# Longer loads in rows of 48 KB, and copies, gelu scaling and row sums on ScalarE, in a one-core adaLN decode kernel

## The chip, the core and the metric

The kernel runs on one NeuronCore of one Trainium2 chip. The core has TensorE (PE in the profile; PEld is its weight load), VectorE (DVE), ScalarE (ACT), GpSimd (POOL) and SyncE (SP), which here does nothing but issue transfers from HBM; 16 DMA engines carry them. PSUM is the memory that TensorE writes, SBUF the working memory of all engines. The metric is the device time of one execution in microseconds (us), the median over several runs. A difference of 2% (7.7 us) is called faster or slower.

## What is computed

One decode step of a transformer block for B = 4 rows of D = 512 values: adaptive layer norm, attention of 32 query heads over 8 cached key/value heads with 4096 positions each, an output projection, a second adaptive layer norm, and a token-mixing MLP with 1792 hidden units. All is fp32.

```python
mod = (_silu(c) @ w_mod).reshape(c.shape[0], 6, 1, -1)
sa, ca, ga, sb, cb, gb = (mod[:, 0], mod[:, 1], mod[:, 2], mod[:, 3], mod[:, 4], mod[:, 5])
h = _layernorm(x, axis=-1) * (1 + ca) + sa
x = x + ga * _A_ref(h, A_k_cache, A_v_cache, A_wq, A_wo)
h = _layernorm(x, axis=-1) * (1 + cb) + sb
x = x + gb * _B_ref(h, B_w1, B_b1, B_w2, B_b2)
...
scores = jnp.einsum("bhqd,bhkd->bhqk", q, k) * (Dh ** -0.5)
p = _softmax(scores, axis=-1)
o = jnp.einsum("bhqk,bhkd->bhqd", p, v)
...
u = jnp.einsum("bsd,sf->bdf", h, w1) + b1
u = _gelu(u)
y = jnp.einsum("bdf,fs->bds", u, w2) + b2
```

The caches hold 4 x 8 = 32 pairs of a key tile K and a value tile V, each 128 partitions by 4096 fp32 values, 16 KB in each partition and 2 MB in all. The kernel reads each once: 128 MB of its 157 MB.

## The kernel before

**Heads.** The unit of work is a "head" i = 0 to 31, a pair of batch row b = i // 8 and key/value head h = i % 8. For head i the score matmuls `s` (L231) read K_i, VectorE takes the row maximum (`m`, L236), TensorE turns it (`pm`, L240), VectorE takes the maximum over the four column groups (`mx`, L245), TensorE spreads it with its sign changed (`pb`, L251), VectorE copies it from PSUM to SBUF (`nm`, L256), and ScalarE computes the exponential with its sum (`p`, L261). VectorE transposes p (L267), TensorE multiplies it with V_i (`pv`, L291), and VectorE copies the product to SBUF (`po`, L314). Then TensorE gathers the head's output (`pt`, L328, called the pick here), multiplies it with the output weights (`pa`, L343), and VectorE adds it up (`acc`, L361).

**The loop.** For i = 0 to 23 a loop runs these steps staggered. Iteration i has, in TensorE's order: the scores of head i+2, the pick, the sums and the projection of head i-1, the turn of the maximum of head i+2, the first half of the values of head i, the spread `pb` of head i+2, and the second half of the values of head i. The pv tile in PSUM has one buffer, and so the values of head i+1 start only when `copy_v(i)` has emptied it; the pick of head i reads that copy. The last eight heads run in an order written out by hand, the string `PLAN`, whose letters are looked up in two tables.

**The mixer.** The MLP of batch row b runs inside the loop while the heads of row b+1 are attended: `Mixer.inner(k)` and `Mixer.outer(k)` with k = i % 8 add a piece to each iteration (i = 8 to 15 for row 0, 16 to 23 for row 1; row 2 is in `PLAN`, row 3 behind it). For k = 3, 4, 5 in `inner`, and k = 2 to 5 in `outer`, `both()` makes one tile of hidden units: `expand` (two VectorE instructions, scale and bias, L442) and `gelu` (one ScalarE instruction of 1024 elements per partition, L506). `inner` stands ahead of the second half of the values and of `copy_v(i)` in the program, `outer` behind. The exponential and gelu need different ScalarE tables, so ScalarE has an ACT_TABLE_LOAD at each change.

**Loads.** All loads go through one queue, SP's. A ring of three slots of 32 KB per partition (`ring`, bufs=3) takes 4 MB loads: `load_first` K0 and K1, then `load_pair(i)` K(i+2) and V(i) side by side in rows of 32 KB. A slot is free when both its tiles are read. In the last stage `PLAN` places the loads (LP, LT, LK, LV, LW). The output weights come in four loads of 2 MB (`wo_p`), the weights of the modulations in three groups (`wmod`).

**Where the last heads fold the gate.** `fold_gate` multiplies eight slices of the output weights with the gate and takes row sums of the result in one VectorE instruction each (L592).

Of the kernel before, what the change touches and what calls it, by code (L numbers as in the profile page):

```python
# [8 lines left out]
F32 = mybir.dt.float32  # L9
AF = mybir.ActivationFunctionType  # L10
OP = mybir.AluOpType
# [13 lines left out]
NARROW = NS - 3  # L25


@with_exitstack
def adaln_decode(ctx: ExitStack, tc: tile.TileContext, small, x, wmod, wq, kk, kv, vv, wo, out):
# [12 lines left out]
    mm = nc.tensor.matmul  # L42
    dv = nc.vector
# [4 lines left out]
    wm01 = ring.tile([P, 2, 4, D], F32, name="wm01", tag="kv")  # L48
    nc.sync.dma_start(wm01, wmod[0])
    nc.sync.dma_start(sm, small)  # L50
    nc.sync.dma_start(xr, x)
    wqt = []
    for k in range(0, 4, 2):
        t = ring.tile([P, 2, HQ * DH], F32, name=f"wq{k}", tag="kv")
        nc.sync.dma_start(t, wq[k // 2])
        wqt += [t[:, 0], t[:, 1]]
    w1, b1, w2 = sm[:, 0:NF], sm[:, NF:2 * NF], sm[:, 2 * NF:3 * NF]
# [33 lines left out]
    wo_p = [wos.tile([P, 2, REP, D], F32, name=f"wo{h}") for h in range(0, HKV, 2)]  # L91
    wo_t = [wo_p[h // 2][:, h % 2] for h in range(HKV)]
# [64 lines left out]
    KT, VT, WM = {}, {}, {}  # L157

    def slots():
        return ring.tile([P, 2, SK], F32, name="kv", tag="kv")  # L160

    def key(t, i):
        KT[i] = t

    def value(t, i):
        VT[i] = t.rearrange("p (j d) -> p j d", d=DH)

    def load_first():
        t = slots()
        nc.sync.dma_start(t, kk)  # L170
        key(t[:, 0], 0)
        key(t[:, 1], 1)

    def load_pair(i):
        t = slots()
        nc.sync.dma_start(t, kv[i])
        key(t[:, 0], i + 2)
        value(t[:, 1], i)

    def load_wo(h):  # L180
        nc.sync.dma_start(wo_p[h // 2], wo[h // 2])

    def load_wm24():
        w = ring.tile([P, 3, 4, D], F32, name="wm24", tag="kv")
        nc.sync.dma_start(w[:, 0:2], wmod[1])
        nc.sync.dma_start(w[:, 2], wmod[2][:, 0])
        for e in range(3):
            WM[2 + e] = w[:, e]

    def load_wm5():  # L190
        t = slots().rearrange("p s (k n) -> p (s k) n", n=D)
        nc.sync.dma_start(t[:, 0:4], wmod[2][:, 1])
        WM[5] = t[:, 0:4]
        return t[:, 4:6]

    def load_key(t, i):
        nc.sync.dma_start(t, kv[i - 2][:, 0])
        key(t, i)

    def load_v(t, i, cuts):  # L200
        value(t, i)
        src = (kv[i][:, 1] if i < NS - 2 else vv[i - NS + 2]).rearrange("p (j d) -> p j d", d=DH)
        for lo, hi in zip(cuts, cuts[1:]):
            nc.sync.dma_start(VT[i][:, lo:hi], src[:, lo:hi])
# [21 lines left out]
    def scores(i):  # L226
        b, h = divmod(i, HKV)
        S[i] = s = ps_s.tile([P, 1024], F32, name=f"s{i}", tag="s")
        for n in range(2):
            for c in range(4):  # L230
                mm(s[32 * c:32 * c + 32, n * 512:(n + 1) * 512], QT[:, b, h, :],  # L231
                   KT[i][:, (n * 4 + c) * 512:(n * 4 + c + 1) * 512], start=True, stop=True)

# [20 lines left out]
    def copy_max(i):  # L254
        nm = wk.tile([P, 1], F32, name="nm")
        dv.tensor_copy(nm, M[i])  # L256
        M[i] = nm
# [27 lines left out]
    def values(i, ks):  # L285
        if ks[0] == 0:
            PV[i] = ps_v.tile([P, 4 * DH], F32, name="pv", tag="pv")
        pT = PL[i][0]
        for k in ks:
            q = k % 4  # L290
            mm(PV[i][32 * q:32 * q + 32, :], pT[:, 128 * k:128 * k + 128:4],  # L291
               VT[i][:, 4 * k:4 * k + 4, :].rearrange("p j d -> p (j d)"), start=(k < 4), stop=(k >= 4))

    def values_narrow(i, ks, pv=None):
        if ks[0] == 0:
            PV[i] = ps_v.tile([P, DH], F32, name="pvn", tag="pv") if pv is None else pv
        pv = PV[i]
        pT = PL[i][0].rearrange("p (k r) -> p k r", r=32)
        top = 32 if i < NS - 1 else 30
        for k in ks:  # L300
            for j in range(4 * k, min(4 * k + 4, top)):
                c = j % 4
                mm(pv[32 * c:32 * c + 32, :], pT[:, j, :], VT[i][:, j, :], start=(k == 0), stop=(j + 4 >= top))  # L303

# [32 lines left out]
    def project(i, pa=None, between=None):  # L337
        b, h = divmod(i, HKV)
        oT = OT[i]
        if pa is None:  # L340
            pa = ps_m.tile([P, D], F32, name="pa", tag="m")
            for g in range(REP):
                mm(pa[32 * g:32 * g + 32, :], oT[:, g:g + 1].to_broadcast([P, 32]), wo_t[h][:, g, :],  # L343
                   start=True, stop=True)
        else:
            for g in range(REP):
                for c in range(4):
                    mm(pa[32 * c:32 * c + 32, :], oT[:, g:g + 1].to_broadcast([P, 32]),  # L348
                       wo_t[h][:, g, c * P:(c + 1) * P], start=(g == 0 and h == HKV - 2),
                       stop=(g == REP - 1 and h == HKV - 1))  # L350
# [105 lines left out]
    class Mixer:  # L456
# [52 lines left out]
        def both(self, u=None):  # L509
            self.expand(u)  # L510
            self.gelu()
# [40 lines left out]
    def finish(b, pg, py, hb, wr):  # L552
        uu = ring.tile([P, 16, D], F32, name="uu", tag="kv")
# [55 lines left out]
    load_first()  # L609
    load_pair(0)  # L610
    load_wo(0)
# [6 lines left out]
    for i in range(NS - HKV):  # L618
        load_pair(i + 1)
        if i in (1, 3, 5):  # L620
            load_wo(i + 1)
        if i == 1:
            load_wm24()
# [25 lines left out]
        if i == 2:  # L649
            for t in range(2, 5):  # L650
                pm = mod(t)
                dst = prep[:, {2: 1, 3: 2, 4: 3}[t]]
                if t == 4:
                    dv.tensor_scalar(dst, pm, 1.0, None, op0=OP.add)
                else:
                    nc.scalar.activation(dst, pm, AF.Copy)
        if i == NS - HKV - 2:
            gate = spread_gate()
# [4 lines left out]
    pve = pgx = pc = ep = spare = slot = None  # L663
    gates = list(range(2 * REP))
    cuts = {NS - 1: (0, 16, 24, 28, 30, 32), NS - 2: (0, 16, 32)}
    last, halves = [(0, 1, 2, 3), (4, 5), (6,), (7,)], [(0, 1), (2, 3), (4, 5), (6, 7)]
    PLAN = """
    a23 v24.0 A23 p23 t25.0 P23 F R v24.1 LP25 G s26 t25.1 M H V24 LP26 Q a24 S26 v25.0 N s27 x A24 f p24 g
    x LP27 m26 S27 P24 m27 X26 X27 b26 B26 e26 x b27 v25.1 c g t26.1 l25 t26.0 B27 s28 V25 c g L25
    v26.0 v26.1 S28 x l26 f a25 L26 V26 A25 x m28 p25 LT X28 e27 c a26 P25 t27.0 A26 b28 s29 f B28 p26 e28  # L670
    LK30 t27.1 S29 P26 v27.0 m29 l27 g LK31 T t28.1 X29 LT t28.0 s30 L27 S30 b29 v27.1 B29 e29 l28 m30 V27
    LV28 L28 a27 g X30 t29.1 t29.0 l29 L29 s31 A27 LV29 b30 p27 x B30 S31 c c m31 e30 P27 X31 v28.0 f LT LV30
    b31 v28.1 B31 f e31 LV31 l30 V28 L30 t30.1 l31 L31 a28 t31.1 A28 p28 v29.0 v29.1 t30.0 f P28 V29 v30.0 a29
    v30.1 A29 LW p29 f v30.2 v30.3 t31.0 P29 g V30 Y y a30 A30 p30 E x v31.0 f v31.1 v31.2 v31.3 V31 z31 a31 I A31 j p31
# [3 lines left out]
             "l": sums, "L": scale, "V": copy_v, "a": pick, "A": copy_o, "P": add_up,  # L678
             "LP": load_pair}
# [4 lines left out]
    for step in PLAN.split():  # L684
# [19 lines left out]
        elif op == "LT":  # L704
            slot = slots()
        elif op == "LK":
            load_key(slot[:, i % 2], i)
        elif op == "LV":
            load_v(slot[:, i % 2], i, cuts.get(i, (0, 32)))
        elif op == "LW":  # L710
            spare = load_wm5()
        elif op == "x":
            mix.expand(spare if mix.n == 6 else None)
# [75 lines left out]
```

## Time and profile before

| | |
|---|---|
| Time, median of 3 runs | 386.43 us (386.31 to 390.96) |
| Span of the profiled execution, first to last instruction | 384.7 us |
| Median run less that span | 1.8 us |
| Mean granted TensorE clock | 0.883 |
| HBM read | 157.32 MB, 409 GB/s over the span |
| Busy: PE, DVE, ACT | 298.7, 198.2, 112.2 us |

The profile is one execution. Its own time as a run is not listed; its span is 1.8 us under the median time, and the work in the argument below is set against the span. Of an engine the page gives busy time and, for each group of instructions, the idle time ahead of them with what ended it. A wait is put down to what came last. The rows that matter are quoted in the prediction.

### The profile page before, as it was taken

Reading aid. Unit: us, or ns where it says so; the run is one execution under the profiler, and the core shown is the slowest. Engines: PE = TensorE matmul, PEld = TensorE weight load, DVE = VectorE, ACT = ScalarE, POOL = GpSimd, SP = SyncE. Lnnn points to the kernel's source line nnn. Section 1 sums busy time; section 2 is a strip of 40 time slices with the busy share of each in tenths; the row PEclk is TensorE's granted clock in tenths of the full one; section 3 lists DMA queues with packets and bytes.
Section 4 is the critical chain, followed back from the end, with each engine's and each line's share of the span. In section 5 each row is a group of like instructions: output and inputs, shape, how many; then the busy total and the mean of one; then the engine's idle time right before and its main releaser. Section 6 shows DMA issues by size and latency. Waiting matters only on the chain.

```text
span 384.7 us, 5604 instructions
## 1 busy us (share of the span) xinstructions
PE 298.7 (78%) x2380; PEld 117.2 (30%) x2380; DVE 198.2 (52%) x407; ACT 112.2 (29%) x144; POOL 7.7 (2%) x33
## 2 busy tenths in 40 slices
PE   0856777866966949979877878788888887999984
PEld 0112122311323313334322222342222343333653
DVE  1130251620451424664866545557665567778757
ACT  1001111121110110212567311124575105657276
POOL 1100000000000000000000000000000000000000
PEclk9989555985695685998999998999999999999999
DMA  8999999999999999999999999999999999999930
GB/s 331 433 433 436 411 453 433 409 432 436 423 441 433 434 436 436 434 436 431 429 425 433 428 433 434 429 433 431 429 434 436 434 436 432 424 417 423 418 122 3
DMA packets 7409, 157.69 MB, mean 410 GB/s; under 512 B 964, under 2 KB 1236, under 8 KB 1496
## 3 DMA queue, kind: packets, MB, share of 16 engines
q1 hardware_dynamic: 7376, 157.33, 95.4%
q8 instruction: 18, 0.29, 0.3%
q14 instruction: 7, 0.06, 0.0%
q10 hardware_dynamic: 8, 0.00, 0.0%
HBM read 157.32 MB, written 0.01 MB: 409 GB/s over the span
## 4 chain that ended last, share of the span: by engine, by line
DMA 60%; PE 29%; DVE 7%; ACT 2%; issue 1%; POOL 0%; SPq 0%; POOLq 0%; DVEq 0%
DMA kv<-in_kv 58%; PE s L231 8%; PE pv L291 7%; PE s L122 2%; PE qs L138 2%; DVE m L236 2%; DVE p L267 2%; DMA sm<-in_small 2%; PE pa L343 2%; PE pt L328 2%; ACT uu L562 1%; PE pb L251 1%; PE pve L303 1%; PE pm L240 1%; PE pgx L348 1%
## 5 line engine op out<-in xcount | busy, mean ns | idle before, releaser
L231 PE MATMUL s<-kv,QT 128*32 128x512 f32 x512 | 75.2, 714 | 38.9 <-DMA kv<-in_kv 37.0
L236 DVE TENSOR_REDUCE m<-s 128x1 f32<-128x1024 f32 x32 | 39.2, 1224 | 96.0 <-PE s L231 95.9
L261 ACT ACTIVATE p<-s,nm 128x1024 f32<-128x1024 f32 x32 | 35.7, 1115 | 180.6 <-DVE nm L256 180.5
L291 PE MATMUL pv<-kv,p 128*32 128x512 f32 x464 | 69.8, 670 | 0.7 <-DMA kv<-in_kv 0.7
L231 PEld LDWEIGHTS s<-kv,QT 128*32 128x32 f32 x512 | 15.8, 123 | 84.0 <-DMA kv<-in_kv 52.5
L328 PEld LDWEIGHTS pt<-g,po 128*128 128x128 f32 x236 | 31.1, 205 | 27.2 <-issue 19.9
L343 PE MATMUL pa<-wo,oT 128*32 128x512 f32 x240 | 34.6, 648 | 4.6 <-DVE oT L335 4.4
L328 PE MATMUL pt<-g,po 128*128 128x4 f32 (+2 forms) x236 | 33.9, 267 | 1.5 <-DVE po L314 1.0
L267 DVE STREAM_TRANSPOSE p<-p 128x1024 f32<-128x1024 f32 x25 | 30.9, 1234 | 0.0
L314 DVE COPY po<-pv 128x512 f32<-128x512 f32 x29 | 20.0, 688 | 16.8 <-PE pv L291 16.7
L245 DVE TENSOR_REDUCE mx<-pm 1x128 f32<-1x512 f32 x32 | 21.3, 669 | 1.1 <-PE pm L240 1.1
L442 DVE TENSOR_SCALAR u<-hb,wr,sm 128x512 f32<-128x512 f32 x40 | 19.9, 541 | 1.9 <-POOL wr L437 1.0
L506 ACT ACTIVATE u<-u 128x1024 f32<-128x1024 f32 x20 | 20.4, 1051 | 1.5 <-DVE u L442 1.4
L361 DVE TENSOR_TENSOR acc<-acc,pa 128x512 f32<-128x512 f32 x26 | 17.8, 686 | 4.3 <-PE pa L343 4.2
L261 ACT ACT_TABLE_LOAD x11 | 14.1, 1283 | 20.3 <-DVE nm L256 20.2
L251 PEld LDWEIGHTS pb<-neg,mx 1*128 1x128 f32 x64 | 10.4, 202 | 28.2 <-DVE mx L245 26.5
L122 PE MATMUL s<-wm,sT 128*4 128x512 f32 x16 | 9.1, 732 | 10.6 <-DVE sT L108 10.6
L506 ACT ACT_TABLE_LOAD x13 | 16.7, 1283 | 0.2
L291 PEld LDWEIGHTS pv<-kv,p 128*32 128x32 f32 x464 | 13.4, 146 | 7.2 <-issue 3.1
L240 PE MATMUL pm<-ident,m 128*1 128x128 f32 x32 | 9.3, 289 | 7.4 <-DVE m L236 3.5
L251 PE MATMUL pb<-neg,mx 1*128 1x1 f32 x64 | 13.1, 271 | 2.1 <-DVE mx L245 2.1
L453 PE MATMUL py<-u,sm 128*32 128x512 f32 x80 | 14.4, 616 | 0.0
(158 smaller groups left out, 214.7 us busy)
## 6 DMA issues: line engine op xcount, KB each, us to landing
kv<-in_kv SPq DMA_DIRECT2D x28, 4096.0 KB, 21.9
wq<-in_wq SPq DMA_DIRECT2D x2, 4096.0 KB, 16.3
wo<-in_wo SPq DMA_DIRECT2D x4, 2048.0 KB
kv<-in_kv SPq DMA_DIRECT2D x4, 2048.0 KB, 20.3
wm<-in_wmod SPq DMA_DIRECT2D x2, 2048.0 KB, 14.8
kv<-in_kk SPq DMA_DIRECT2D x1, 4096.0 KB
kv<-in_vv SPq DMA_DIRECT2D x3, 1024.0 KB
wm<-in_wmod SPq DMA_DIRECT2D x1, 1024.0 KB
```

The lines of the kernel that those rows point to most:

```text
L231: mm(s[32 * c:32 * c + 32, n * 512:(n + 1) * 512], QT[:, b, h, :], KT[i][:, (n * 4 + c) * 512:(n * 4 + c + 1) * 512], start=True, stop=True)
L236: dv.tensor_reduce(M[i], S[i], axis=AX.X, op=OP.max)
L245: dv.tensor_reduce(mx, M[i].rearrange("o (c r) -> o r c", c=4).unsqueeze(1).to_broadcast([1, 4, 32, 4]), axis=AX.X, op=OP.max)
L251: mm(pb, M[i].rearrange("o c r -> o (c r)"), neg1, start=True, stop=True)
L261: nc.scalar.activation(p, S[i], AF.Exp, bias=M.pop(i), accum_out=l)
L267: dv.transpose(PL[i][0], PL[i][0])
L291: mm(PV[i][32 * q:32 * q + 32, :], pT[:, 128 * k:128 * k + 128:4], VT[i][:, 4 * k:4 * k + 4, :].rearrange("p j d -> p (j d)"), start=(k < ...
L314: dv.tensor_copy(PV[i], pv)
L328: mm(pt, po[:, c * DH:(c + 1) * DH], sel.unsqueeze(1).to_broadcast([P, m, REP]), start=(c == 0), stop=(c == n - 1))
L343: mm(pa[32 * g:32 * g + 32, :], oT[:, g:g + 1].to_broadcast([P, 32]), wo_t[h][:, g, :], start=True, stop=True)
L442: dv.tensor_scalar(u[:, e, :], hb, wr[:, j:j + 1], b1[:, j:j + 1], op0=OP.mult, op1=OP.add)
L506: nc.scalar.activation(u, u, AF.Gelu_apprx_tanh)
```

## The change

**Loads.** The ring becomes one tile of six 16 KB tiles (`RING`), and a list made by `queue()` gives the order of the loads. `kk` (K0, K1) is followed by 14 loads `kvk` of three tiles each in rows of 48 KB: by turns K(m+2), V(m), K(m+3), and V(m+1), K(m+4), V(m+2), with m = 0, 3, ..., 18. They cover V0 to V20 and K2 to K22. Then come seven pairs of 32 KB rows, K30, K31 and V28 to V31 one by one, and the last modulation weights. A load is issued as soon as the program has passed the last reader of each tile that it overwrites: `advance(name)` is called behind the last reader. The ring thus holds two loads of three tiles where it held three loads of two.

**Weights.** The output weights come in two loads of 4 MB instead of four of 2 MB. Modulation weights 0 and 1, and later 2 to 4, are loaded into the place of output weights that come behind them, so they no longer take a ring slot. The matmuls of modulations 2 to 4 (`mod`) move from the end of iteration 2 to the end of iteration 1.

**Engines.** `copy_max` (all heads), `copy_v` (heads 0 to 23) and the first `add_up` of each batch row move from VectorE to ScalarE. `both()` loses its two VectorE instructions; ScalarE does scale, bias and gelu in two instructions of 512. `fold_gate` becomes a VectorE multiply of 1024 per partition for the first four calls and a ScalarE copy with a row sum for all eight.

```diff
-    ring = ctx.enter_context(tc.tile_pool(name="ring", bufs=3))
+    ring = ctx.enter_context(tc.tile_pool(name="ring", bufs=1))
...
+    RING = ring.tile([P, 6, SK], F32, name="kv")
+    wo_t = wos.tile([P, HKV, REP, D], F32, name="wo")
+    wm01, wm24 = wo_t[:, 0:2], wo_t[:, 4:7]
...
+    def queue():
+        q = [entry(["K0", "K1"], kk)]
+        for n in range(NT):
+            m = n // 2 * 3
+            names = [f"V{m + 1}", f"K{m + 4}", f"V{m + 2}"] if n % 2 else [f"K{m + 2}", f"V{m}", f"K{m + 3}"]
+            q.append(entry(names, kvk[n]))
+        for i in range(NP, NS - 4):
+            q.append(entry([f"K{i + 2}", f"V{i}"], kv[i - NP]))
...
+        q.insert(2, ("wo", "M0", wo_t[:, 0:4], wo[0]))
+        q.insert(4, ("wo", None, wm24, wm2))
+        q.insert(6, ("wo", "M2", wo_t[:, 4:8], wo[1]))
+        return q
...
+    def advance(name=None):
+        read.add(name)
+        while LOADS:
...
+                if any(h not in read for h in held[p:p + n]):
+                    return
...
     def copy_max(i):
         nm = wk.tile([P, 1], F32, name="nm")
-        dv.tensor_copy(nm, M[i])
+        nc.scalar.activation(nm, M[i], AF.Copy)
...
     def copy_v(i):
         pv = PV[i]
         PV[i] = wk.tile(list(pv.shape), F32, name="po")
-        dv.tensor_copy(PV[i], pv)
+        if i < NS - HKV:
+            nc.scalar.activation(PV[i], pv, AF.Copy)
+        else:
+            dv.tensor_copy(PV[i], pv)
...
-            dv.tensor_copy(ACC[b], pa)
+            nc.scalar.activation(ACC[b], pa, AF.Copy)
...
-        def both(self, u=None):
-            self.expand(u)
-            self.gelu()
+        def both(self):
+            u = up.tile([P, 2, D], F32, name="u")
+            js = (2 * self.n, 2 * self.n + 1)
+            for e, j in enumerate(js):
+                nc.scalar.activation(u[:, e], self.hb, AF.Gelu_apprx_tanh, bias=b1[:, j:j + 1],
+                                     scale=self.wr[:, j:j + 1])
+            self.done.append((u, js))
+            self.n += 1
...
     def fold_gate(gate, es):
-        for e in es:
-            w = wo_t[HKV - 2 + e // REP][:, e % REP]
-            dv.tensor_tensor_reduce(w, w, gate, 1.0, 0.0, OP.mult, OP.add, rowsum[:, e:e + 1])
+        for n in es:
+            if n < REP:
+                w = wo_t[:, HKV - 2 + n // 2, n % 2 * 2:n % 2 * 2 + 2]
+                dv.tensor_mul(w, w, gate.unsqueeze(1).to_broadcast([P, 2, D]))
+            w = wo_t[:, HKV - 2 + n // REP, n % REP]
+            nc.scalar.activation(w, w, AF.Copy, accum_out=rowsum[:, n:n + 1])
...
-        load_pair(i + 1)
-        if i in (1, 3, 5):
-            load_wo(i + 1)
-        if i == 1:
-            load_wm24()
...
-        if i == 2:
+        if i == 1:
             for t in range(2, 5):
...
-    x LP27 m26 S27 P24 m27 X26 X27 b26 B26 e26 x b27 v25.1 c g t26.1 l25 t26.0 B27 s28 V25 c g L25
+    x m26 S27 P24 m27 X26 X27 b26 B26 e26 x b27 v25.1 c g t26.1 l25 t26.0 B27 s28 V25 c g L25
```

ScalarE's order in the iterations with a mixer piece, before: the exponential `p` and the gelu `u` take turns, with a table load ahead of each.

```order
L506 ACT_TABLE_LOAD
L506 ACTIVATE u<-u 128x1024 x2
L261 ACT_TABLE_LOAD
L261 ACTIVATE p,l<-s_1088,nm 128x1024
L506 ACT_TABLE_LOAD
```

The same place after the change:

```order
L271 ACTIVATE nm<-pb 128x1
L276 ACT_TABLE_LOAD
L276 ACTIVATE p,l<-s_1493,nm 128x1024
L535 ACT_TABLE_LOAD
L535 ACTIVATE u<-hb,sm,wr 128x512 x2
L334 ACTIVATE po<-pv 128x512
L535 ACTIVATE u<-hb,sm,wr 128x512 x2
```

The copy `nm` now stands ahead of the exponential, and the copy `po` of the values stands behind the exponential, a table load and the two gelu instructions of `inner`.

TensorE's order of the same iterations before, with the engine that each row waits for (DMAHW is a load):

```order
L231 MATMUL s_1023<-kv,QT 32x512 [waits DMAHW0_49]
L231 MATMUL s_1023<-kv,QT 32x512 x7
L328 MATMUL pt<-g_122,po 128x4 [waits DVE_49]
L328 MATMUL pt<-g_122,po 128x4 x3
L275 MATMUL pl<-g_122,l 128x4 [waits Activation_49]
L343 MATMUL pa<-wo_129,oT 32x512 [waits DVE_49]
```

and after:

```order
L245 MATMUL s_1493<-kv,QT 32x512 x8
L350 MATMUL pt<-g_121,po 128x4 [waits Activation_49]
L350 MATMUL pt<-g_121,po 128x4 x3
L290 MATMUL pl<-g_121,l 128x4
L365 MATMUL pa<-wo,oT 32x512 [waits DVE_49]
```

The pick `pt`, which waited for VectorE's copy, now waits for ScalarE's (Activation).

SP's queue from the first key load on, before (up to the first long run of pairs):

```order
L170 DMA kv<-in_kk 128x8192
L176 DMA kv<-in_kv 128x8192
L181 DMA wo_128<-in_wo 128x4096
L176 DMA kv<-in_kv 128x8192 x2
L181 DMA wo_129<-in_wo 128x4096
L185 DMA wm_337<-in_wmod 128x4096
L186 DMA wm_337<-in_wmod 128x2048
```

and after:

```order
L210 DMA kv<-in_kk 128x8192
L210 DMA kv<-in_kvk 128x12288
L192 DMA wo<-in_wo 128x8192
L210 DMA kv<-in_kvk 128x12288
L192 DMA wo<-in_wm 128x6144
L210 DMA kv<-in_kvk 128x12288
L192 DMA wo<-in_wo 128x8192
L210 DMA kv<-in_kvk 128x12288 x11
L210 DMA kv<-in_kv 128x8192 x7
```

The 45 transfers of the new queue carry the same bytes as the 55 of the old one.

More of the change, by code (lines that the diff above doesn't have):

```diff
@@ L155, in adaln_decode @@
     nc.scalar.activation(prep[:, 0], px, AF.Copy)
[L157 to L204, printed above, removed]
+    KT, VT, WM = {}, {}, {2 + e: wm24[:, e] for e in range(3)}
+    held, read = [("Q", 0), ("Q", 0), ("Q", 1), ("Q", 1), None, None], {None, ("Q", 0), ("Q", 1)}
@@ new lines, in adaln_decode @@
+    LOADS, at = queue(), [4]
+    def advance(name=None):
+        read.add(name)
+        while LOADS:
+            kind, names, *rest = LOADS[0]
+            if kind == "wo":
+                if names not in read:
+                    return
+                nc.sync.dma_start(*rest)
+            else:
+                n, p = len(names), at[0]
+                if any(h not in read for h in held[p:p + n]):
+                    return
+                for k, nm in enumerate(names):
+                    t, i = RING[:, p + k], int(nm[1:])
+                    if nm[0] == "K":
+                        KT[i] = t
+                    elif nm[0] == "V":
+                        VT[i] = t.rearrange("p (j d) -> p j d", d=DH)
+                    else:
+                        WM[i] = t.rearrange("p (k n) -> p k n", n=D)[:, 0:4]
+                held[p:p + n] = names
+                at[0] = (p + n) % 6
+                if names[0] == "W5":
+                    nc.sync.dma_start(WM[5], rest[0])
+                elif len(names) > 1:
+                    nc.sync.dma_start(RING[:, p:p + n], rest[0])
+                elif names[0][0] == "K":
+                    nc.sync.dma_start(RING[:, p], rest[0])
+                else:
+                    cs = cuts.get(i, (0, 32))
+                    v = rest[0].rearrange("p (j d) -> p j d", d=DH)
+                    for lo, hi in zip(cs, cs[1:]):
+                        nc.sync.dma_start(VT[i][:, lo:hi], v[:, lo:hi])
+            LOADS.pop(0)
@@ L552, in finish @@
     def finish(b, pg, py, hb, wr):
-        uu = ring.tile([P, 16, D], F32, name="uu", tag="kv")
+        uu = RING[:, 4:6].rearrange("p s (k n) -> p (s k) n", n=D)
         for js in ((0,), (1,), (2, 3, 4), (5, 6, 7), (8, 9, 10), (11, 12), (13,)):
```

77 lines of the change are left out of this document (42 added, 35 removed).

## The prediction

> **What bounds the kernel now.** I read the page's slices and queues first, then the chain of waits, then who waits late in the program.
>
> ```profile
> span 384.7 us, 5604 instructions
> ...
> DMA  8999999999999999999999999999999999999930
> GB/s 331 433 433 436 411 453 433 409 432 436 423 441 433 434 436 436 434 436 431 429 425 433 428 433 434 429 433 431 429 434 436 434 436 432 424 417 423 418 122 3
> ...
> q1 hardware_dynamic: 7376, 157.33, 95.4%
> ...
> kv<-in_kv SPq DMA_DIRECT2D x28, 4096.0 KB, 21.9
> ```
>
> The 16 DMA engines are full from the first slice to the 39th at some 433 GB/s. The loads are the bound, and bytes don't change; what can be won on them is small, and each microsecond in which the queue stands empty is lost. The chain of waits gives the pace:
>
> ```profile
> 201.31 1.97 PE s L231 x16
> ...
> 208.57 21.85 DMA kv<-in_kv
> 230.47 3.32 PE s L231 x16
> ...
> 260.73 1.97 PE s L231 x16
> ...
> 289.74 1.97 PE s L231 x16
> ```
>
> These starts of scores wait for a pair's landing and lie three heads apart: 29.0 us, 9.67 for a head, 4.84 for a tile of 2 MB. Last, the waits of TensorE from 289 us to 372 us:
>
> ```profile
> PE s L231 <- DMA kv<-in_kv: 2.2, 2, 1.6
> ...
> PE pv L291 <- DMA kv<-in_kv: 0.7, 2, 0.5
> ```
>
> Of these 2.9 us, 1.6 are the wait at 289.74 itself. Behind it TensorE waits 1.3 us for loads until the end: whatever makes it late at head 24 makes the end late, less 1.3.
>
> **The new wait.** In iterations 11, 12, 13 and 19, 20, 21 ScalarE copies the values only behind `inner`'s gelus, and the next pick needs that copy. TensorE's part at full clock (timeline; pick, spread, second half of the values, MLP matmuls):
>
> ```profile
> 201.31 1.92 PE L231 MATMUL s<-kv,QT 128*32 128x512 f32 x16 [1.70 <-DMA kv<-in_kv]
> 203.16 1.06 PE L328 MATMUL pt<-g,po 128*128 128x4 f32 x8
> ...
> 206.07 1.10 PE L291 MATMUL pv<-kv,p 128*32 128x512 f32 x8
> 207.11 0.38 PE L251 MATMUL pb<-neg,mx 1*128 1x1 f32 x2
> 207.42 1.10 PE L291 MATMUL pv<-kv,p 128*32 128x512 f32 x8
> 208.33 1.04 PE L453 MATMUL py<-u,sm 128*32 128x512 f32 x8
> ```
>
> Scores to pick 1.85; pick to the end of the spread 207.49 - 203.16 = 4.33; pick to the last read of V 5.36. ScalarE's part, by groups and two timeline rows:
>
> ```profile
> L261 ACT ACTIVATE p<-s,nm 128x1024 f32<-128x1024 f32 x32 | 35.7, 1115 | 180.6 <-DVE nm L256 180.5
> L506 ACT ACT_TABLE_LOAD x13 | 16.7, 1283 | 0.2
> ...
> L261 ACT ACTIVATION_READ_ACCUMULATOR p<-s,nm 128x1 f32 x32 | 6.2, 193 | 0.0
> ...
> L218 ACT ACTIVATE ym<-pm 128x512 f32<-128x512 f32 x3 | 1.8, 597 | 7.8 <-PE pm L215 7.8
> L557 ACT ACTIVATE uu<-hb,sm,wr 128x512 f32<-128x512 f32 x2 | 1.5, 806 | 0.1
> ...
> L416 ACT ACTIVATE sd<-ph,epsc 128x1 f32<-128x1 f32 x1 | 0.3, 261 | 0.5 <-PE ph L737 0.5
> ```
>
> ```profile
> 267.19 1.28 ACT L261 ACT_TABLE_LOAD   x1 [4.59 <-DVE nm L256]
> ...
> 268.48 1.11 ACT L261 ACTIVATE p<-s,nm 128x1024 f32<-128x1024 f32 x1
> ```
>
> Copy of the maximum 0.26 (nearest row: one column, 261 ns), table load 1.28, exponential with its sum 1.31, table load 1.28, two scaled gelus 1.5 (their rows overlap), copy of the values 0.60, hand-overs 0.1: 6.33. The load of the exponential's table stood idle until `nm` was there; the order after has it behind `nm` too, so it stays in the ring of waits. Pick to pick takes 4.33 + 6.33 = 10.66 us, against 9.67 of the stream. Behind the waiting pick stand the projection, the turn of the maximum and the next values on TensorE; behind `nm` on ScalarE everything that ScalarE does, which is why the turns are serial. `outer`'s gelus come behind the copy, in the shadow of TensorE's 4.33.
>
> The Trainium skill, ScalarE: Activation LUTs, section "What ACT_TABLE_LOAD costs", has a drain of some 1380 ns beside the 1283 ns of every switch. The trace doesn't agree: 267.19 + 1.28 is 268.47, and the exponential starts at 268.48. By the page each turn would take 2.8 us more, a rival below.
>
> **The ring.** At the median a pair landed 21.9 us after its issue, 9.7 of them its own: it was issued with 12.2 us of work still queued. Two loads of three tiles leave less; behind a load that SP holds back stand all later loads. What a late issue costs:
>
> ```profile
> 0.72 0.39 SPq L49
> ...
> 1.18 7.60 DMA sm<-in_small
> ```
>
> The first slice (9.62 us) moved 331 of 433 GB/s, so 2.27 us of it are empty; less 0.72, 1.5 us lie between issue and first bytes. The first load and `small` are 2.13 MB, 4.9 us; 2.2 + 4.9 = 7.1, but `small` landed at 8.78: a landing comes 1.7 us behind the last byte.
>
> Now along the stream, first mixer. The score at 201.31 waits for K15 and V13. Afterwards [K14,V12,K15] lands one tile earlier, at 196.5, and head 14's scores start there. Picks: 198.3; spread's end 202.7, copy 209.0 = next pick; 219.7 the third; V14 is read at 225.0. The load after the next two goes over V14. Those two end in bytes at 196.5 + 29.0 - 1.7 = 223.8; its own start at 226.5: an empty queue for 2.7 us.
>
> Second mixer, without that gap. 260.73 is K21's landing with V19; afterwards [K20,V18,K21] lands at 255.9. Head 20's scores, once possible at 251.1, start there; head 21's 8.8 us later (251.1 to 259.8 before), 264.7. V19 comes with the next load, 255.9 + 14.5 = 270.4. Spread's end 271.8, copy and pick 278.2, then 288.8 and 299.5. Before, that last pick stood here:
>
> ```profile
> 291.59 1.05 PE L328 MATMUL pt<-g,po 128*128 128x4 f32 x8
> ```
>
> So it is 7.9 us late; with the gap 10.6; less 1.3 of slack, 9.3 at the end.
>
> **The clock.** In each turn TensorE has 1.85 + 5.36 + 0.95 = 8.2 us of work in 10.66 and idles 2.5. Idle times and granted clock before:
>
> ```profile
> 172.23 3.37 PE L231 MATMUL s<-kv,QT 128*32 128x512 f32 x16 [1.88 <-DMA kv<-in_kv]
> ...
> 230.47 3.26 PE L231 MATMUL s<-kv,QT 128*32 128x512 f32 x16 [2.46 <-DMA kv<-in_kv]
> ```
>
> ```profile
> 141.00:154.70 13.70, 11.45 (x53) 4.21 (x57) 4.04 (x7) 0.73 (x1) 0.00 (x0) 0.50 1.03 442
> ...
> 171.80:175.20 3.40, 2.97 (x16) 0.60 (x16) 0.02 (x1) 0.00 (x0) 0.00 (x0) 0.50 0.96 414
> ...
> 229.80:233.20 3.40, 2.73 (x16) 0.59 (x16) 0.00 (x0) 0.00 (x0) 0.00 (x0) 0.50 1.00 434
> ```
>
> Behind idle times of 1.88 and 2.46 us the clock (third column from the end) was 0.50 for 3.4 us, and elsewhere for 13.7 at a stretch; 1.70 us (201.31) did nothing. At that clock pick to spread's end is longer:
>
> ```profile
> 122.43 1.87 PE L328 MATMUL pt<-g,po 128*128 128x4 f32 x8
> ...
> 128.69 0.58 PE L251 MATMUL pb<-neg,mx 1*128 1x1 f32 x2
> ```
>
> 129.27 - 122.43 = 6.84, 2.5 more. Six turns: 0 to 15 us; half of them slow, 7.5. The two-load ring also has longer idle stretches and no reserve at that clock: in the plain heads, 120 to 190 us, a load must be issued 14.5 - 1.7 - 1.5 = 11.3 us behind a landing, its last reader ends at 7.2 + 1.9 = 9.1 at full clock and, if the span from pick on stretches by 6.84/4.33, at some 14.4: up to 3 us of empty queue for each drop there, and two or three drops: 0 to 9, I take 2.5. Together 10, between 0 and 24.
>
> The Trainium skill, TensorE: Matmul & The Clock Gate, Part 1, has the clock halve after at least one idle window of some 3.4 us. The rows show halving after 1.88 us without work. By the page the 2.5 us of a turn would leave the clock alone, and the sum would lack the 7.5; that is the first rival.
>
> **What costs nothing or little.** Fewer, longer transfers: the stream holds about 433 in slices full of 32 KB rows; 436, its best common slice, over 336 us would be 2.3 us; between -2.3 and 0, I take 0, since neighbouring slices differ by more than any row length shows. Dropping VectorE's `po`, `nm` and expand frees an engine that in the mixers is not the last. In the last stage the folds' row sums add 8 x 0.79 to ScalarE, beside VectorE's relief; a wait for either is under a microsecond, between -1 and 1, I take 0. The modulation matmuls one iteration earlier, and the output weights behind them, have the 6 MB load between them in the queue as cover; without it, its length above what TensorE needs, a few microseconds at most. The key load K0, K1 no longer waits, but queues behind loads that fill 28 us anyway: 0.
>
> **Sum.** 384.7 + 9.3 + 10 = 404.0; the median of the runs lies 1.8 above the span: 405.8, forecast 406 us, 5% slower. By about 2%, 7.7 us, a measurement of this kernel can tell a change from none.
>
> **Rivals.** *The clock holds.* Then 384.7 + 9.3 + 1.8 = 396. For it: 54.6 us at 1.00 in this stretch before, with waits of 1.6 and 1.7. Against it: 2.5 is above 1.88. *The copy comes in time, not slower.* If the exponential's table load ran while TensorE works, a turn would be 9.4, under the 9.67 that decides; TensorE then regains the late start of head 20 (4.8 us at 1.4 a head), and the time is 386 to 389. Against it: the 4.59 us of idling ahead of that load. *A slow clock throughout.* With all the turns slow and a gap at every drop, 395.7 + 15 + 9 = 420. For it: 13.7 us at half clock three times over before. *Drain at a table switch:* six turns of 2.8 us more, 396 + 17 = 413 and with the clock's share 423. *Faster:* were ten fewer transfers worth 2 us each, 366; against it, the queue that never empties. The Trainium skill, DMA: Bandwidth & Descriptors, "Anatomy of one DMA", has that fixed 2 us for a single transfer; the steady 433 GB/s shows it hidden in a queue.
>
> **Chances.** Forecast (400 to 416): 0.70. Clock holds (394 to 400): 0.11. In time: 0.07. Slow throughout (over 416): 0.08. Drain: 0.03. Faster: 0.01. From 395 to 416 holds all but 0.2. Slower: 0.70 + 0.10 + 0.08 + 0.03 = 0.91; same 0.07 + 0.01 = 0.08; faster 0.01.
>
> **What would show it.** Right: TensorE's pick in the mixer iterations waits some 2.5 us for ScalarE's `po`, picks lie 10.7 us apart or more; GB/s falls below 433 in slices near 225 us; more slices at half clock. Wrong: no such wait; 433 GB/s throughout, with the end unmoved; the exponential's table load not idle behind `nm`; or a lateness that appears only in the last stage.

## The result and the profile after

The changed kernel takes 417.86 us (median of 4 runs, 416.31 to 419.01) where the kernel before took 386.44 on the same chip (386.31 to 390.96): 1.080 times as long, 95% interval 1.076 to 1.084. It is slower by 31.4 us; the forecast was 19.6 slower, 406 us, with 416 as the upper end of its range. The profiled execution, the fastest of the four, took 416.31 with a span of 414.5, so its span is set against the 384.7 of before: 29.8 more.

From the page of after, TensorE's clock, the transfers by slice (one slice is now 10.36 us) and the load queue:

```profile
PEclk9988558555886879679995996859878989699999
...
GB/s 333 430 449 436 428 428 455 412 425 441 349 437 436 386 404 386 441 324 408 427 447 413 281 441 414 360 447 352 428 433 317 391 386 365 427 430 419 221 2 3
...
q1 hardware_dynamic: 5936, 157.33, 90.4%
```

The stream that was never empty now has holes from the 11th slice on. The deepest, 281 in slice 23 (228 to 238 us), is worth (433 - 281) / 433 x 10.36 = 3.6 us. The digits of the clock fall in the same part of the program. The view by cores gives the mean granted clock, 0.883 before:

```profile
core 0: 414.5 us, clock 0.814
```

If the clock is either 1.00 or 0.50, that is 90 us at half before and 154 after: (1 - 0.883) / 0.5 x 384.7, and the same with 0.814 and 414.5.

What TensorE waited for, after (total, times, longest). The third row is the wait that the prediction described; the last one, for a copy moved to ScalarE, it did not have:

```profile
PE pv L306 <- DMA kv<-in_kvk: 20.1, 4, 10.0
PE s L245 <- DMA kv<-in_kvk: 17.5, 5, 6.6
PE pt L350 <- ACT po L334: 11.2, 6, 2.5
...
PE pm L255 <- ACT acc L381: 2.6, 1, 2.6
```

In the kernel before, TensorE waited for loads just as long:

```profile
PE s L231 <- DMA kv<-in_kv: 37.0, 19, 6.5
```

So the 37.6 us of the first two rows of after are no measure of the loss. Before, the stream ran full during these waits.

The chain of waits of after (start, duration, what) from the plain heads to the last turn of the second mixer:

```profile
107.35 1.72 PE s L245 x16
...
114.36 1.76 PE s L245 x16
116.14 24.29 DMA kv<-in_kvk
140.47 3.12 PE s L245 x16
...
153.62 19.15 DMA kv<-in_kvk
172.81 3.64 PE s L245 x16
...
186.12 17.40 DMA kv<-in_kvk
203.56 1.97 PE s L245 x16
...
209.97 1.28 ACT L276
211.26 1.21 ACT p L276 x2
...
228.51 1.07 PE pt L350 x8
...
266.40 2.77 PE s L245 x16
...
317.16 1.05 PE pt L350 x8
```

Read it as a loop: a load lands, its last reader ends, the next load goes out behind that reader, lands, and so on. The stream brings the six tiles of a round in 29.0 us; here 140.47 to 172.81 is 32.3 and 172.81 to 203.56 is 30.8. From a landing to the issue that it lets go takes 153.62 - 140.47 = 13.2 us, with scores of 3.12. The same stretch ran ahead of the first long wait, at full clock, from 107.35 to 116.12: 8.8 us, with scores of 1.72.

Where the 29.8 us arise, by four marks along this chain, beside what the prediction had for each stretch:

| Stretch | Late at its end | Added | Priced at |
|---|---|---|---|
| to the landing of K14, V12, K15 (203.56 for 196.5) | 7.1 | 7.1 | 2.5 (plain heads) |
| to the landing of K20, V18, K21 (266.40 for 255.9) | 10.5 | 3.4 | 2.7 (gap in the queue) |
| to the last pick that waits for ScalarE (317.16 for 291.59 before) | 25.6 | 15.1 | 7.9, and 7.5 for all turns at half clock |
| to the end (414.5 for 384.7) | 29.8 | 4.2 | -1.3 (slack) |

196.5 and 255.9 are the prediction's landings without any lateness. The right-hand column adds up to 19.3. Of the 10.5 us that it lacks, 4.6 arise in the plain heads and 5.5 behind the last pick.

### The profile page after: what moved, and what is told of

It reads as the page before. It is cut to its first block, busy times and chain, and to the rows that moved or that the text cites. A ratio compares the mean times of both kernels' runs of the same rounds, so it can differ in the third digit from the quotient of the medians.

```text
span 414.5 us, 5581 instructions
## 1 busy us (share of the span) xinstructions
PE 317.3 (77%) x2380; PEld 124.7 (30%) x2380; DVE 162.4 (39%) x307; ACT 144.0 (35%) x234; POOL 7.7 (2%) x33
## 3 DMA queue, kind: packets, MB, share of 16 engines
q1 hardware_dynamic: 5936, 157.33, 90.4%
## 4 chain that ended last, share of the span: by engine, by line
DMA 37%; PE 32%; issue 14%; ACT 10%; DVE 5%; SPq 1%; POOL 0%; POOLq 0%; ACTq 0%
DMA kv<-in_kvk 20%; DMA wo<-in_wm 9%; PE s L245 9%; DMA kv<-in_kk 8%; PE pv L306 8%; PE pa L365 4%; PE pt L350 4%; ACT u L535 2%; ACT p L276 2%; DVE m L251 2%; ACT L535 2%; ACT L276 2%; DVE p L282 2%; PE pb L266 1%; PE pm L229 1%
## 5 line engine op out<-in xcount | busy, mean ns | idle before, releaser
L306 PE MATMUL pv<-kv,p 128*32 128x512 f32 x464 | 81.5, 777 | 20.1 <-DMA kv<-in_kvk 20.1
L271 ACT ACTIVATE nm<-pb 128x1 f32<-128x1 f32 x32 | 5.5, 171 | 170.0 <-PE pb L266 169.9
L350 PE MATMUL pt<-g,po 128*128 128x4 f32 (+2 forms) x236 | 36.0, 276 | 11.7 <-ACT po L334 11.2
L350 PEld LDWEIGHTS pt<-g,po 128*128 128x128 f32 x236 | 33.3, 217 | 37.1 <-ACT po L334 19.9
L365 PE MATMUL pa<-wo,oT 128*32 128x512 f32 x240 | 39.0, 728 | 3.5 <-DVE oT L357 3.4
L282 DVE STREAM_TRANSPOSE p<-p 128x1024 f32<-128x1024 f32 x25 | 30.8, 1233 | 0.0
L266 PEld LDWEIGHTS pb<-neg,mx 1*128 1x128 f32 x64 | 12.0, 233 | 34.6 <-DVE mx L260 24.0
L535 ACT ACTIVATE u<-hb,sm,wr 128x512 f32<-128x512 f32 x28 | 21.2, 804 | 0.1
L123 PE MATMUL s<-wo,sT 128*4 128x512 f32 x16 | 9.2, 738 | 10.4 <-DVE sT L109 10.4
L334 ACT ACTIVATE po<-pv 128x512 f32<-128x512 f32 x24 | 14.1, 588 | 4.6 <-PE pv L306 4.5
L255 PEld LDWEIGHTS pm<-ident,m 128*1 128x1 f32 x32 | 2.5, 79 | 41.3 <-DVE rl L295 29.0
```

Source lines behind the costliest of these rows:

```text
L266: mm(pb, M[i].rearrange("o c r -> o (c r)"), neg1, start=True, stop=True)
L282: dv.transpose(PL[i][0], PL[i][0])
L350: mm(pt, po[:, c * DH:(c + 1) * DH], sel.unsqueeze(1).to_broadcast([P, m, REP]), start=(c == 0), stop=(c == n - 1))
L535: nc.scalar.activation(u[:, e], self.hb, AF.Gelu_apprx_tanh, bias=b1[:, j:j + 1], scale=self.wr[:, j:j + 1])
```

## Experiments

Four causes were set against each other. A: ScalarE copies the values behind the gelus, so the turns are long. B: two loads in the ring are too few. C: rows of 48 KB move slowly. D, later: TensorE's work as such. A1 was added after the first four runs: A and B both lose through TensorE's clock, and feed each other. All times stand beside runs of the kernel before on the same chip, 386.4 to 386.5 us.

**Taking the change apart.** `copy_dve` puts one copy back:

```diff
-        if i < NS - HKV:
-            nc.scalar.activation(PV[i], pv, AF.Copy)
-        else:
-            dv.tensor_copy(PV[i], pv)
+        dv.tensor_copy(PV[i], pv)
```

> The changed kernel with one thing undone: the copy of the values (po) stands on VectorE again for every head, so no pick waits for ScalarE. Loads of three tiles, maximum copy, scaled gelus, row sums stay on ScalarE. Theory A (the copy behind the gelus on ScalarE makes the turns of the mixer iterations too long, and the late turns empty the queue and drop the clock): the waits of pt for po are gone, picks 9.7 us apart, time 386 to 394. Theory B (the ring of two 48 KB loads has too little reserve for any kernel, the clock drops, and the copy adds little): 404 to 415. Theory C (rows of 48 KB are slower to move): 405 to 417, with loads that take longer than 14.5 us although they were issued in time.

Measured: 400.14 us (ratio 1.035, 1.030 to 1.039). The waits for `po` are gone, and so are 17.7 us, but 13.7 are left, outside what A had and below what B had.

`loads_only` puts all engine moves back (`copy_max`, `copy_v`, the first sum, `both`, `fold_gate`) and keeps the loads:

> Only the change of the loads: rows of 48 KB, four-head output weights, the ring without pools, in the changed kernel; every engine move is undone (copy of the maximum, of the values and of the first sum, scaled gelus and row sums stand where they stood before). Theory A (ScalarE's copy is the cause): 385 to 392, within 2% of before. Theory B (two-load ring): 400 to 412, with waits of TensorE for kvk loads of some 10 to 20 us in all from 107 us on. Theory C (48 KB rows are slow): 400 or more, loads longer than 14.5 us with a full queue.

Measured: 397.29 us (1.026, 1.020 to 1.033), between A and B. Its chain of waits shows the loop by itself:

```profile
103.80 19.36 DMA kv<-in_kvk
...
123.20 1.94 PE pv L306 x8
...
125.66 1.87 PE pv L306 x8
127.53 2.67 PE s L245 x16
...
133.06 1.02 PE pv L306 x8
...
134.41 1.07 PE pv L306 x8
...
135.49 18.36 DMA kv<-in_kvk
...
166.39 18.32 DMA kv<-in_kvk
...
200.15 18.87 DMA kv<-in_kvk
...
232.07 18.29 DMA kv<-in_kvk
...
263.03 18.62 DMA kv<-in_kvk
```

From 103.80 to 263.03 the loop takes 159.2 us for five rounds, 31.8 each, against the stream's 29.0. A round is 18.3 of load behind an empty queue (14.5 of its own) and 12.3 to 15.4 of work from landing to issue. In that work the first values take 1.94 and 1.87; the same instructions take 1.02 and 1.07 a few microseconds later, when the clock has come back. Without the slow start the work would be, as an estimate from these rows, some 12.3 - 0.9 - 0.8 - 0.9 = 9.7 (scores 1.76 for 2.67), the round 28.0, under 29.0, and no load late. So the loss feeds itself: a late load leaves TensorE idle, the idle clock slows the reading of that load, and so the next load is late.

`engines_only` is the other half, on the kernel before: its loads and its ring of three, with all the engine moves.

> Only the engine moves, on the kernel before: its loads of pairs and ring of three pairs stay; copy of the maximum, of the values, of the first sum, scaled gelus and row sums as in the change. Theory A: the pick waits for ScalarE's po six times, some 2.5 us each; picks 10.7 us or more apart in the mixer iterations; with three pairs in the ring the loads have 12 us of reserve, so only the lateness itself and some clock is lost: 388 to 396. Theory B (two-load ring alone): 385 to 388. If the engine moves are the whole loss whatever the ring: 410 to 418.

Measured: 396.96 us (1.025, 1.020 to 1.031), 1 us above what A had; the interval reaches down to the 2% that counts as slower. Its picks and waits in the first mixer:

```profile
196.61 1.36 PE L331 MATMUL pt<-g,po 128*128 128x4 f32 x8 [2.50 <-ACT po L315]
209.04 1.05 PE L331 MATMUL pt<-g,po 128*128 128x4 f32 x8 [1.97 <-ACT po L315]
220.56 1.40 PE L331 MATMUL pt<-g,po 128*128 128x4 f32 x8 [2.49 <-ACT po L315]
```

They are 12.4 and 11.5 us apart. Loads alone cost 10.8 us, engines alone 10.5, both 31.4: 10 more than the sum.

`gelu_late` is the changed kernel with the same instructions and one other order:

```diff
             elif k <= 5:
-                self.both()
...
         def outer(self, k):
+            if 3 <= k <= 5:
+                self.both()
```

> The changed kernel with the copy of the values on ScalarE as changed, but the scaled gelus of the inner part of a mixer iteration issued behind that copy instead of ahead of it; the same instructions, one order. Theory A: ScalarE's part of a turn loses 1.5 us of gelu and a table load of 1.28 ahead of the copy, 10.7 becomes 7.9, under the stream's 9.67; waits of pt for po gone: 386 to 394. Theory B (ring of two loads) or C (48 KB rows): no better than 404.

Measured: 401.86 us (1.042, 1.037 to 1.048); no wait for `po` among TensorE's waits. It lies between A (up to 394) and B (from 404). It wins 16.0 us, nearly as much as putting the copy back; 15.4 are left, of which the loads alone have 10.8.

**TensorE made light.** The next four kernels have TensorE's large matmuls read the upper halves of the numbers, as in the scores:

```diff
+    def top(t):
+        return t.bitcast(mybir.dt.bfloat16).rearrange("p (n e) -> p n e", e=2)[:, :, 1]
...
-                mm(s[32 * c:32 * c + 32, n * 512:(n + 1) * 512], QT[:, b, h, :],
-                   KT[i][:, (n * 4 + c) * 512:(n * 4 + c + 1) * 512], start=True, stop=True)
+                mm(s[32 * c:32 * c + 32, n * 512:(n + 1) * 512], top(QT[:, b, h, :]),
+                   top(KT[i][:, (n * 4 + c) * 512:(n * 4 + c + 1) * 512]), start=True, stop=True)
```

> A control for the next three: the kernel before, with TensorE's large matmuls (scores, values, pick, projection, first MLP blocks) reading only the upper 16 bits of each number, as bfloat16; the same loads, waits and instructions elsewhere, and a coarser result. TensorE's part of a head becomes a fraction of what it was, so its clock hardly matters. The loads bound this kernel in every theory: 380 to 387, 433 GB/s in nearly all slices.

> The change of the loads alone (run loads_only: 397), with the light matmuls of the control (upper 16 bits, coarser result). Theory A1 (the loop of landing, half-clock matmuls, late issue feeds itself: a wait of 5 us drops the clock, the dropped clock makes the next issue 3 us later): no queue left empty, 381 to 387, level with its control. Theory B1 (two loads in the ring are too few whatever TensorE's speed, since issue to landing takes 18.3 us and VectorE's and ScalarE's steps stand in the loop too): 392 or more, with kvk loads 30.5 us or more apart by pairs. Theory C (48 KB rows move slowly): 392 or more with the queue full.

> The engine moves alone (run engines_only: 397 by the median, 393.5 to 398.5), with the light matmuls of the control. Theory A1: what is left is ScalarE's ring, 6.3 us of ScalarE and some 3.5 of TensorE and hand-overs, about the 9.67 of the stream: 381 to 388, level with its control. If ScalarE's part alone were the loss, without the clock: 392 or more, picks still 11 us apart in the mixer iterations.

> The whole change with the light matmuls of the control. Theory A1 (both parts lose through TensorE's clock and feed each other): 382 to 392, of the 31 us that the change costs at most 9 are left. Theory B2 (the two parts lose by themselves, ScalarE's 6 us in series and the two-load ring): 400 or more. The waits of pt for ScalarE's po stay in both, longer than 2.5 us, since TensorE is at the pick earlier.

Measured: 386.95 (control), 388.33, 387.78 and 388.11 us. Of the 31.4 us 1.7 are left (1.0042, 1.0027 to 1.0057). The mean clock is 0.57 to 0.59, at half nearly throughout, and no longer matters. ScalarE's turn has not become shorter. Wait and turn in `after_bf`:

```profile
PE pt L354 <- ACT po L337: 26.6, 14, 4.2
```

```profile
201.35 0.17 ACT L274 ACTIVATE nm<-pb 128x1 f32<-128x1 f32 x1 [2.82 <-PE pb L269]
```

```profile
207.41 0.27 PE L354 MATMUL pt<-g,po 128*128 128x4 bf16 x4 [4.23 <-ACT po L337]
...
217.76 0.27 PE L354 MATMUL pt<-g,po 128*128 128x4 bf16 x4 [4.23 <-ACT po L337]
```

TensorE waits longer for `po` than in the changed kernel (26.6 us for 11.2), ScalarE's part still takes 6.1 us, the turns are 10.35 us apart, above 9.67; and it costs nearly nothing: the next two picks follow after 8.24 and 6.41 us (226.00 and 232.41), so a light TensorE regains the lateness. A wait in the trace is thus no loss by itself. C falls too: `loads_bf` moves the same 48 KB rows. Its span and queue:

```profile
span 386.7 us, 4056 instructions
...
q1 hardware_dynamic: 5936, 157.33, 95.0%
```

That is 367 us of transfers, as before (95.4% of 384.7).

**Work kept, clock taken out.** The light matmuls take away TensorE's work as well as the price of its slow clock. `after_eq` and `loads_eq` issue the light matmuls twice, so that at half clock they take about what the full ones take at full clock; the second copy of the scores is the same matmul again, that of the values multiplies with zeros:

```diff
+            mm(PV[i][32 * q:32 * q + 32, :], top(none), top(VT[i][:, 4 * k:4 * k + 4, :].rearrange("p j d -> p (j d)")),
+               start=(k < 4), stop=(k < 4))
             mm(PV[i][32 * q:32 * q + 32, :], top(pT[:, 128 * k:128 * k + 128])[:, ::4],
```

> The whole change with TensorE's work sized so that at half clock it takes about what the full numbers take at full clock: the matmuls of run after_bf (upper 16 bits, coarser result), those of scores, values, projection and MLP blocks issued twice (the second copy of no effect on the result), the pick with six extra ones, the sum and the spread of the maximum in 16 bits too. So the drop of the clock is taken out and the work is left in. Theory A1 (the clock is the larger part): 393 to 400, the loss left is ScalarE's ring and the start of the gaps; the prediction's own sum without its clock term is 396. Theory D (the clock is no matter, TensorE's work as such is too much beside ScalarE's): 405 or more. If 386 to 390: ScalarE's ring costs nothing without the clock, and the prediction's 9.3 us were the clock's too.

> The change of the loads alone with TensorE's work sized in the same way. Theory A1: the loop from landing to the next issue takes 18.3 us of load and some 9.6 of work, 27.9, under the 29.0 of three heads, so no queue runs empty for long: 386 to 390. Theory D: as loads_only, 394 or more.

Measured: 391.41 us (1.011, 1.006 to 1.016) and 390.18 (1.010, 1.007 to 1.014). The whole change, with TensorE's work but without the price of its half clock, costs 5.0 us; so up to 26.4 of the 31.4 are the clock's. This is an upper bound, for two reasons. The clock rose now and then in these runs too, and the work was then lighter than meant:

```profile
PEclk9969655555665657655557656555786857887899
```

And not all of the work is kept. At half clock the doubled scores take 1.90 us (`loads_eq`, 138.34 to 140.24), like the full ones at full clock (1.92), but the pick takes 0.43 for 1.05, the sums 0.17 for 0.36 and the spread 0.18 for 0.38. A turn of `after_eq` is thereby 9.62 us, under the stream's 9.67:

```profile
198.57 0.32 PE L361 MATMUL pt<-g,po 128*128 128x4 bf16 x6 [0.56 <-ACT po L343]
...
208.19 0.30 PE L361 MATMUL pt<-g,po 128*128 128x4 bf16 x6 [3.74 <-ACT po L343]
```

With the full work at full clock a turn takes 10.42 us, as shown below. For five turns that is some 4 us of missing work, so as an estimate the clock's share is some 22 us. No run keeps the work exactly and takes only the clock out.

`after_eq` lies just under the range of A1 and far from D; `loads_eq` lies at the upper end of A1 (386 to 390).

**Without the long turn.** `pairs_dve` keeps of the change only the ring without pools, the output weights in two loads and the earlier modulation; all loads are pairs again.

> What is left of the change when every load is a pair again (32 KB rows in a six-tile ring, so three loads) and every engine move is undone: the ring without pools, output weights in two loads of four heads, modulation one iteration earlier. By all theories the stream bounds it: 384 to 388. Below 385.6 it would be a version that beats the kernel before, by fewer transfers; the profile of before leaves little to win, since its queue never empties.

Measured: 391.27 us (1.010, 1.007 to 1.013), a miss: this rest costs 1% by itself. Its transfers have one hole, in slice 9 (77 to 87 us):

```profile
GB/s 329 433 433 433 432 433 420 447 330 431 433 432 433 432 433 433 432 433 432 433 432 433 429 433 432 433 433 432 430 432 433 432 433 429 415 423 424 417 112 4
```

(433 - 330) / 433 x 9.68 = 2.3 us. At this place the modulation matmuls run and the load of output weights waits for them; that this wait makes the hole wasn't tried by itself. The profiled run took 388.96 us, 2.5 above the kernel before, which the hole nearly covers; what the median's other 2.3 us are is open. The changed kernel has no such hole at this place (412 to 441 in slices 8 to 10), nor has `loads_only` (421 to 445), so these 4.8 us cannot be taken as a part of the 31.4.

`engines_late` is `engines_only` with the order of `gelu_late`: all engine moves, three loads in the ring, the inner gelus behind the copy.

> The engine moves on the kernel before (its pairs and its ring of three loads), with one order changed: the inner gelus behind the copy of the values on ScalarE. What the runs so far say: without the turn of 10.4 us TensorE idles less between spread and pick, keeps its clock, and three loads have reserve: no wait of pt for po, 385 to 389, a version that keeps the moves at no loss (run engines_only: 397). It can hardly beat the kernel before, whose queue is never empty. If the moves cost by themselves (ScalarE's copies of the maximum and of the values in the ring of every head): 392 or more.

Measured: 388.22 us (1.0039, 1.0013 to 1.0064). Two of its picks in the first mixer:

```profile
203.01 1.06 PE L331 MATMUL pt<-g,po 128*128 128x4 f32 x8
212.68 1.06 PE L331 MATMUL pt<-g,po 128*128 128x4 f32 x8
```

9.67 us apart, with no wait. The order alone wins 8.7 of the 10.5 us. None of the kernels beats the one before.

## Why the prediction was half right

**Right: what bounds, and ScalarE's turn.** The forecast was 4.33 + 6.33 = 10.66 us from pick to pick. The timeline of after, at full clock:

```profile
205.41 1.05 PE L350 MATMUL pt<-g,po 128*128 128x4 f32 x8
...
209.37 0.38 PE L266 MATMUL pb<-neg,mx 1*128 1x1 f32 x2
...
215.83 1.61 PE L350 MATMUL pt<-g,po 128*128 128x4 f32 x8 [2.49 <-ACT po L334]
```

Pick to the spread's end 4.34, from there to the next pick 6.08, together 10.42. The forecast's timeline has five picks that wait for this copy, some 2.5 us each. In the trace they are those at 215.83, 228.51, 293.00, 304.53 and 317.16, with waits of 2.49, 0.54, 2.50, 2.49 and 2.19 us; the sixth wait of the table, 0.96 us at 335.00, lies behind them. `copy_dve` and `gelu_late` show that the place of this copy is worth 16 to 18 us. The drain at a table switch was rightly left out: the load at 209.97 takes 1.28, and the exponential starts at 211.26. Two readings of the trace of before were slightly off, and the sum doesn't rest on them: the transfer engines were full to the 38th slice, not the 39th, and the four starts of scores lie 29.0 to 30.3 us apart; the 29.0 is right as the pace of the bytes.

**Right: the gap in the queue near 225 us.** 2.7 us forecast; it came in slice 23, 3.6 us, later by the lateness brought along. The load over V14 went out at 233.75, right behind the end of V14's reading at 233.69, for which the forecast had 225.0.

**Right in sign, wrong in size: the clock.** The term was 10 us between 0 and 24; `after_eq` puts it at up to 26.4, some 22 by the estimate above. The rest of the sum had 9.3 us; `after_eq` shows 5.0, with those 4 us of work missing. Its pieces were right one by one. A slow turn was priced 2.5 us longer; 215.83 to 228.51 is 12.7, 2.3 more. A plain head's stretch from landing to issue was put at 9.1 at full clock and 14.4 when slow; 8.8 and 13.2 were measured. What failed is the value taken in the step "up to 3 us of empty queue for each drop there, and two or three drops: 0 to 9, I take 2.5". The drops came as counted: behind waits of 6.17, 3.26 and 6.56 us the readings that start at 125.15, 140.47 and 172.81 ran at 0.50, and only the fourth long wait left the clock alone. The first and the fourth:

```profile
125.15 1.94 PE L306 MATMUL pv<-kv,p 128*32 128x512 f32 x8 [6.17 <-DMA kv<-in_kvk]
...
203.56 1.92 PE L245 MATMUL s<-kv,QT 128*32 128x512 f32 x16 [2.82 <-DMA kv<-in_kvk]
```

Counted back from 196.5 in steps of 29.0, the loads of the chain landed 1.9 us late at 140.43, 5.3 at 172.77 and 7.0 at 203.52. Each round thus added 1.8 to 3.4 us, about what the prediction had for a drop; the 2.5 that it took for all of them is less than the price of one, and 7.1 were gone in the place of 2.5. The kernel before had its drops in the same stretch, behind waits of 6.45, 5.20 and 1.88 us, but with three loads in the queue they left no hole. With two, a drop can make the next load late, and the late load makes the next idle stretch. Behind 203.56 the pieces met the sum up to the last pick: 3.4 + 15.1 = 18.5 us, for 2.7 + 7.9 + 7.5 = 18.1.

The windows of before and after say the same (columns: busy times, then the clock, the DMA share and GB/s):

```profile
90.00:200.00 110.00, 89.60 (x582) 33.29 (x574) 53.24 (x100) 21.02 (x28) 1.34 (x3) 0.80 1.00 432
200.00:320.00 120.00, 96.25 (x767) 39.19 (x771) 71.93 (x141) 43.41 (x51) 2.62 (x6) 0.99 1.00 432
```

```profile
90.00:200.00 110.00, 89.33 (x584) 34.05 (x582) 40.44 (x70) 23.95 (x46) 1.33 (x3) 0.77 0.96 403
200.00:320.00 120.00, 98.03 (x644) 37.56 (x640) 44.05 (x75) 58.03 (x85) 1.31 (x3) 0.82 0.94 396
```

In the plain heads the clock was hardly better before (0.80 for 0.77), yet the stream ran at 432 for 403. Behind 200 us it used to recover to 0.99 and now stays at 0.82.

**Wrong: the slack at the end.** The sum took off 1.3 us for waits for loads, and had nothing else for this stretch. These waits did go: behind 317.16 TensorE waits for no load, so the low slices 31 to 34 (311 to 352 us, 317, 391, 386 and 365) held up none of its work. But it needed 5.5 us more than before for its own work and for ScalarE. Its clock was 0.59 from 318.0 to 322.2, 0.62 from 336.0 to 340.0 and 0.59 from 353.3 to 360.9 us; before, the same work ran at full clock in the first two stretches and at 0.72 from 325 to 331. And the `pm` at 353.13 waited 2.57 us for the first sum `acc`, before 0.88 us for VectorE. On ScalarE this copy starts at 352.50, behind a table load of 1.28 and a gelu of 1.06 us: the same fault of order as with the copy of the values. That is up to 1.7 of the 5.5 us; how the rest divides over the slow stretches is open.

**Costs nothing: nearly right.** Longer rows cost and win next to nothing (`loads_bf`, 1.4 us over its control). The engine moves, with the gelus in the right place and three loads in the ring, cost 1.7 us (`engines_late`). What the earlier modulation and the weights' loads cost was taken as 0; `pairs_dve` says some 5 us for them in a ring of pairs, while the changed kernel shows no hole at their place.

**The rivals.** *Slow clock throughout* was the nearest in time (420 for 417.86), with a chance of 0.08. Its gap at every drop is what happened; its slow turns came only in part (10.42, 12.68, 10.43, 11.53 and 12.63 us). That its time fits so well is partly luck, since it too had nothing for the 5.5 us at the end. *The clock holds* (396) lies 5 us above `after_eq`'s 391. The Trainium skill, TensorE: Matmul & The Clock Gate, Part 1, has the clock halve after at least one idle window of some 3.4 us; the trace doesn't agree: the 2.49 us ahead of the pick at 215.83 were enough.

## What to carry to other kernels

A ring has reserve only if landing to issue, plus issue to landing with an empty queue, is shorter than the time in which the stream brings the bytes of the ring, and this must hold with TensorE at half clock, since a late load can cause exactly that. Here it was 9.7 + 18.3 = 28.0 us at full clock (an estimate), against 29.0, and 31.8 as measured. Where a copy that another engine waits for goes to an engine with other work, it belongs ahead of that work, as far as its input is there: the same instructions in another order were worth 16 us here. Price two changes that eat the same reserve together, not as a sum: 10.8 and 10.5 us alone were 31.4 together.

## What the hardware did unasked

Half clock outlasted the idle time by far, and the length of the idle time alone doesn't tell whether it comes: 2.82 us without work ahead of 203.56 left the clock at 1.00 up to 213.4 us, 2.49 us ahead of 215.83 halved it. TensorE in the windows before and after the pick at 215.83:

```profile
213.40:215.80 2.40, 0.00 (x0) 0.00 (x0) 1.22 (x1) 2.39 (x5) 0.00 (x0) 1.00 1.18 512
216.10:219.40 3.30, 3.30 (x18) 1.88 (x17) 1.38 (x3) 1.09 (x2) 0.00 (x0) 0.51 1.07 462
219.40:226.30 6.90, 6.90 (x35) 1.80 (x35) 1.28 (x2) 3.80 (x5) 0.00 (x0) 0.50 0.94 406
```

After 2.4 us without work it stayed at half for the 10.2 us of the second and third row, in which TensorE was busy without a break. The Trainium skill's page named above, in the same part, has it come back after at least one busy window of some 3.4 us; here it took three times that.

A load of three tiles that was issued into an empty or nearly empty queue took 17.4 us from issue to landing in the changed kernel (186.12) and 18.3 to 18.9 us in most rounds of `loads_only`, where its bytes take 14.5. So 2.9 to 4.4 us come on top, around the prediction's 1.5 + 1.7. And the same 157 MB kept the transfer engines busy for longer in two runs in which the queue ran empty: 90.4% of 414.5 us, 375 us, after, and 370 us in `loads_only` (93.2% of 397.1), against 367 before and in `loads_bf`. Which packets were slow, and why, is open.
